# Block products in the first pass over d_ff for groups 3, 4 and 5

## The chip, the cores and the metric

The kernel runs on one core of one Trainium2 chip. The metric is the time of one execution on the device in microseconds. Each time shown is of one whole execution; the profile is of one further execution, whose span is counted from its first instruction to its last. The engines are TensorE (PE, with its weight loads as PEld), VectorE (DVE), ScalarE (ACT), GpSimd (POOL) and SyncE (SP), which issues all of this kernel's DMAs.

## The reference

The first half is an attention over 4 batches, 8 heads, 768 positions and 64 columns per head. A query sees the keys less than 16 positions away (local part) and, in the same softmax, 24 summaries of the whole sequence: the maximum of the keys and the mean of the values of each block of 32 positions, with log(32) added to the scaled score. The heads are joined to x, 3072 tokens by 512 columns. The second half is a feed-forward layer:

```
h = x @ w_in                                      # 512 -> 2048
g = np.maximum(h, 0.0) + np.log1p(np.exp(-np.abs(h)))   # softplus
return (g @ w_out).astype(np.float32)             # 2048 -> 512
```

q, k, v and w_in come with eight times their plain spread. w_in and w_out reach the kernel as 64-bit numbers, which it turns into float32 on the chip.

## The kernel before

**Precision.** A float32 matrix is kept as two parts in the type float32r, high and low (a rounded copy and the rest). A product of two such matrices is three matmuls, high x high, high x low and low x high (TERMS).

**Tokens and groups.** The 3072 tokens are twelve chunks of 256 (CH), two to a group: six groups of 512 tokens (x = 0 to 5). d_ff is sixteen blocks of 128 (f = 0 to 15), of which the first eight are one half (HALF). Only half of the weights lies in SBUF at a time, so the phases are: groups 0 to 4 with the first half, group 5 with the first half and then the second, and groups 4 to 0 with the second. After a first pass, po (512 tokens by 512 columns in PSUM) goes to DRAM as "part", and x as "raw"; the second pass loads both again (attended, reload).

**Attention** of a chunk (attention, L605) goes by two pairs of heads: scores (PE, L629), mask and maximum (DVE, L642), exponential (ACT, L650), inverse sums (DVE), normalise (POOL, DVE or ACT, L663, L666), transpose by blocks on DVE (L696) and through DRAM (L704, L708), values (PE, L727, into xo, a PSUM bank of the ring "ph"). For groups 1 to 4 xo is copied to a block r (L739), kept in DRAM, and split into high and low parts of whole x (prepare_whole, L813 and L820). For groups 0 and 5 it is split straight from the bank (L757, L761). The attention of a group stands in the order beside the products of the one or two groups ahead of it.

**Plain products.** hidden (L1036) makes h of one f: 12 matmuls of 512 columns, in two tasks h0 and h1 (L1045). The result has one of the two PSUM banks of the ring "ph".

**Block products.** hidden_pair (L1062) makes h of two f at once. x is seen as 2 by 2 blocks (chunk by half of d_model), and so is the w_in of the two f. Seven products of blocks, six matmuls of 256 columns each (L1085; a11, s3, s2, s1, a12, s4, a22), take the place of eight; seven combinations on DVE (L1095) and a copy of one product (p1, L1104 or L1105) put them together in two banks, z and y, which the pair holds both. It needs seven operands of x: blocks 0, 1, 3 and x12's and others' differences (prepare, L834: less is a subtraction, L797 or L798; split is a high part, L782, and a low part, L789), in places x0 to x2 (two buffers each) and x3 to x6 (one each). And it needs four sums of blocks of w_in (sums_of_weights, L968: joined L985, combined L993 to L996, high L1009, low L1016), in places s0 to s3.

**After h**: high part of softplus (gh, L1147), exact softplus in place in the bank (L1151), rest (gl, L1155), and the projection to po (L1162), per f 8 matmuls with gh and 4 with gl, or, for the first and last f of a pass, 3 for each of four groups of 128 tokens.

**Where block products are used before**: "pairs = f0 > 0" (L1124), so in the second passes of groups 4 to 0 alone. The sums of w_in are made for the second half only (arrive, L1281).

**Order.** Every task (a matmul chain, an operation on an engine, a DMA) is declared with what it reads and writes; SEQUENCE, a list of task numbers written out by hand in the file, gives the order in which all are issued (Order.issue), and each engine and SP's queue run their tasks in that order. A letter behind a number picks another engine for a task (ways). Buffers of the ring "t" (two), and banks of "ph" (two), are given out in the order of the sequence.

The first task numbers of the sequence are those of the start: constants, 40 matmuls on ident, the first keys and values (declare_first, declare_first_values, L412), where six loads of v (L423) go through the ring "gh" of four buffers and are summed on PE (L428).

Of the kernel before, what the change touches and what calls it, by code (L numbers as in the profile page):

```python
# [147 lines left out]
0 3 4 162 43 1 5 6 51 7 44 8 9 10 11 12 13 14 15 16 17 18 19 20 21 22 23 24 25 26 27 28 29 30 31 32 33 153 45 47 68  # L148
154a 158a 34 155 163a 64 46 52 156 53 55 164 2 157 165 167a 72 54 35 57 189 69 36 159 59 160a 161 49 73 48 37 86 313
61 166 56 74 171 87 190 38 39 168 75 58 40 191 88 41 60 104 62 100 76a 172a 50 152 321a 180 192 176a 77 79 66 316 65  # L150
173 174 63 67 169 42 78 108 71 175 80 170 70 177 314 315 185 194 101 109 89 312 193 110 122 123 81 324 208 198 181a
103 90b 124 107 105 343 111 82 195 84 344 182 209a 91 102 136 106 196a 112a 346 183 199 184 92 93 94 95 325 83 213
178a 197 85 342 113 125 326 372 345 96 186 210 211 114 179 351 212 138 115 116 98 117 99 97 376 126b 127 317 118 120
327 214 200a 129 128 215a 130 354 137 217 131 373 246 218 380 328 329 134 330 140 132 121 141 355 133 320 119 135 201
247 319 356 248 390 255 249 392 393 331 223a 357 187 389 334 332 318 374 322 333 391 202 204 250 256 257 188 262 203
139 258 323 216a 358 259 359 263 227 219a 377 264 251 269 270 252 205 146a 398a 271 384 360 378 265 206a 401 375 220
272 253 266 228a 335 347 350 232 353 221 254 260 402 336 273 381 361 420 229 423 421 143 276 362 363 348 230 364 419
385 403 277 349 422 283 352 338 261 222 379a 382 404 386 284 231 428 278 236 279 237 207a 280 405b 267 431 285 286 365
233 406 407 234 515 366 516 224 268 274 287 432 433 238a 368a 235 383a 290 387a 394 291 408 396 388 225 292 149a 434
239 240 520a 517 297 241 410 411 400 397 340 409 275 298 226 435a 436 242 523 299 293 395 281 399 693 542 243 294 282  # L160
# [73 lines left out]
def kernel(  # L234
# [639 lines left out]
    def weights(pair):  # L874
# [6 lines left out]
        for outer, which in tiles:  # L881
# [81 lines left out]
            )  # L963


    s_bufs = {}

    def sums_of_weights(f):  # L968

# [365 lines left out]
```

## Time and profile before

| | us |
|---|---|
| three runs | 633.65, 633.3, 628.66 |
| median | 633.3 |
| the profiled execution, whole | 630.05 |
| its span | 628.3 |
| mean granted clock of TensorE | 0.983 of full speed |

The page of the profile gives the busy time of each engine, and the chain that ended last followed back from the last instruction. A window of the profile gives the busy time of each engine in a stretch of the span, so a stage can be read by itself. The boundaries of the stages, from PE's instructions in the order of the sequence: group 0's products begin at 51.9 us, group 1's at 110.1, group 2's at 164.0, group 3's at 215.0, group 4's at 270.8, group 5's at 323.8 and its second half at 362.6; the block products of group 4 begin at 406.0, of 3 at 446.4, of 2 at 490.4, of 1 at 530.8 and of 0 at 572.2. A matmul's duration in the profile is longer than the spacing of matmuls, as they overlap; the spacing is read from the chain of waits, which counts them.

### The profile page before, as it was taken

The numbers are of one execution on the slowest core, as the hardware profiler recorded it, in microseconds if no ns is written. First come the engines' busy times: TensorE is split into PE (matmuls) and PEld (weight loads), VectorE is DVE, ScalarE is ACT, GpSimd is POOL, SyncE is SP. The second block draws the span as 40 slices with busy tenths as digits, with TensorE's granted clock in tenths as the row PEclk, the third lists the DMA queues.
The fourth block names the chain that finished last, engine by engine and source line by source line (L and its number), as shares of the span: only waits on it lengthen the run. The fifth ranks groups of instructions, "written<-read, shape, count | busy, mean of one in ns | idle before, by whom it ended". The sixth has DMA issues, their size and how long they took to land.

```text
span 628.3 us, 12022 instructions
## 1 busy us (share of the span) xinstructions
PE 609.2 (97%) x4452; PEld 508.9 (81%) x4452; DVE 388.0 (62%) x998; ACT 328.0 (52%) x809; POOL 162.0 (26%) x145
## 2 busy tenths in 40 slices
PE   8769999999999999999999999999999999999997
PEld 7557777788888878877888888899889899898995
DVE  5887997764457454535427979764557557655442
ACT  2898895965766676456526677441323122222220
POOL 3325435132213043002003443490111403002000
PEclk9868999999999999999999999999999999999999
DMA  9998887989998887885634632103122050030301
GB/s 303 265 272 268 254 264 233 262 261 231 272 263 253 259 268 220 254 236 158 212 116 155 222 127 84 34 34 118 51 76 78 17 185 1 35 100 1 104 32 67
DMA packets 88955, 104.39 MB, mean 166 GB/s; under 512 B 27489, under 2 KB 67009, under 8 KB 88129
## 3 DMA queue, kind: packets, MB, share of 16 engines
q1 hardware_dynamic: 88896, 103.62, 54.5%
q8 instruction: 35, 0.57, 0.4%
q14 instruction: 24, 0.19, 0.1%
HBM read 73.92 MB, written 27.26 MB: 161 GB/s over the span
## 4 chain that ended last, share of the span: by engine, by line
PE 85%; DMA 8%; SPq 3%; ACT 1%; DVE 1%; issue 1%; DVEq 0%; POOL 0%; POOLq 0%; ACTq 0%
PE po L1162 40%; PE ph L1045 21%; PE hx L1085 9%; PE hy L1085 7%; PE xo L727 3%; PE sc L629 3%; DMA raw<-w_in_dram 2%; DMA k<-kT_dram 2%; DMA squares<-tb 2%; PE warm L1236 2%; DMA kf<-kT_dram 1%; DMA q<-qT_dram 1%; DMA v<-v_hp_dram 1%; SPq L708 1%; SPq L523 1%
## 5 line engine op out<-in xcount | busy, mean ns | idle before, releaser
L1162 PE MATMUL po<-w,gh 128*128 128x512 f32 x768 | 204.2, 394 | 0.0
L1162 PEld LDWEIGHTS po<-w,gh 128*128 128x128 f32 x768 | 141.4, 188 | 30.6 <-issue 0.6
L1045 PE MATMUL ph<-xw,w 128*128 128x512 f32 x672 | 163.9, 395 | 2.1 <-DVE gl L1155 2.0
L1045 PEld LDWEIGHTS ph<-xw,w 128*128 128x128 f32 x672 | 125.6, 188 | 32.5 <-DVE gl L1155 2.8
L1162 PE MATMUL po<-w,gl 128*128 128x512 f32 x384 | 116.6, 397 | 0.0
L1162 PEld LDWEIGHTS po<-w,gl 128*128 128x128 f32 x384 | 70.9, 188 | 15.9 <-issue 0.5
L650 ACT ACTIVATE sp<-sp,nm 128x120 f32<-128x120 f32 x192 | 73.1, 382 | 5.9 <-DVE nm L642 5.7
L1147 ACT ACTIVATE gh<-hx 128x512 fp32r<-128x512 f32 x20 | 12.0, 599 | 114.9 <-DVE hx L1095 114.9
L948 POOL TENSOR_TENSOR t<-t,raw 128x1024 int32<-128x1024 int32 (+1 forms) x20 | 42.4, 2122 | 98.8 <-DVE t L934 28.4
L1155 DVE TENSOR_TENSOR gl<-ph,gh 128x512 fp32r<-128x512 f32 x56 | 38.0, 684 | 40.8 <-ACT ph L1151 39.3
L1147 ACT ACTIVATE gh<-ph 128x512 fp32r<-128x512 f32 x56 | 33.5, 598 | 53.4 <-PE ph L1045 48.5
L789 POOL TENSOR_TENSOR x<-r,x 128x512 fp32r<-128x512 f32 x18 | 24.5, 1370 | 82.0 <-ACT x L782 32.2
L642 DVE CUSTOM_DVE_ANT_0 sp<-sc,added 128x120 f32<-128x120 f32 x192 | 40.8, 277 | 4.9 <-PE sc L629 3.9
L663 POOL TENSOR_TENSOR sp<-sp,ss 128x960 f32<-128x960 f32 x10 | 18.4, 1843 | 87.6 <-DVE ss L658 62.8
L650 ACT ACTIVATION_READ_ACCUMULATOR sp<-sp,nm 128x1 f32 x192 | 36.0, 187 | 0.0
L1085 PE MATMUL hx<-x,sw 128*128 128x256 f32 x240 | 35.4, 283 | 0.0
L1085 PE MATMUL hx<-x,w 128*128 128x256 f32 x240 | 35.1, 282 | 0.0
L1085 PEld LDWEIGHTS hx<-x,w 128*128 128x128 f32 x240 | 32.8, 189 | 1.9
L696 DVE STREAM_TRANSPOSE tb<-sp 128x1024 f32<-128x1024 f32 x20 | 24.8, 1242 | 15.2 <-POOL sp L663 7.9
L1085 PE MATMUL hy<-x,sw 128*128 128x256 f32 x240 | 33.2, 282 | 0.0
L1151 ACT ACTIVATE ph<-ph 128x512 f32<-128x512 f32 x56 | 32.8, 591 | 0.0
L1085 PEld LDWEIGHTS hx<-x,sw 128*128 128x128 f32 x240 | 31.7, 189 | 0.5
(108 smaller groups left out, 821.6 us busy)
## 6 DMA issues: line engine op xcount, KB each, us to landing
squares<-tb SPq DMA_DIRECT2D x20, 512.0 KB
pT<-squares SPq DMA_DIRECT2D x80, 128.0 KB
raw<-w_out_dram SPq DMA_DIRECT2D x16, 512.0 KB
kf<-kT_dram SPq DMA_DIRECT2D x16, 384.0 KB
raw<-w_in_dram SPq DMA_DIRECT2D x6, 1024.0 KB
q<-qT_dram SPq DMA_DIRECT2D x20, 256.0 KB
raw<-r SPq DMA_DIRECT2D x20, 256.0 KB
part<-ob SPq DMA_DIRECT2D x10, 512.0 KB
```

What stands on the lines that cost most here:

```text
L629: nc.tensor.matmul(unit(g * NU + h * NPAIR + i)[r * QW:(r + 1) * QW, k0:k1], lhsT=q[rows, w * QW:(w + 1) * QW], rhs=k[rows], start=True, s ...
L642: nc.vector.tensor_tensor_reduce(out=sp()[:, n], in0=unit(n), in1=added()[:, kinds.index((lows[w], lows[w + 1]))], scale=-SCALE, scalar=FL ...
L650: nc.scalar.activation(sp()[:, n], sp()[:, n], AF.Exp, bias=nm()[:, n:n + 1], scale=-1.0, accum_out=ss()[:, n:n + 1],)
L696: nc.vector.transpose(out=tb().rearrange("p k (u q) -> p u k q", q=SQ), in_=tiles.sp().rearrange("p u (k q) -> p u k q", q=SQ),)
L789: engine.tensor_tensor(to(1), a(), to(0).bitcast(F32), op=ALU.subtract)
L948: nc.gpsimd.tensor_tensor(a, a, word(0, I32), op=ALU.add)
L1045: nc.tensor.matmul(ph(), lhsT=lhs(part, cc), rhs=xw[cc][0]()[:, xw[cc][1], a], start=cc == 0 and n == 0, stop=cc == NCC - 1 and n == 2,)
L1085: nc.tensor.matmul(to()[:, half], lhsT=lhs(wa, cc), rhs=of_x(xa)[:, cc * CH:(cc + 1) * CH], start=cc == 0 and m == 0, stop=cc == NG - 1 an ...
L1147: nc.scalar.activation(gh(), all_of(), AF.Softplus)
L1151: nc.scalar.activation(all_of(), all_of(), AF.Softplus)
L1155: nc.vector.tensor_sub(out=gl(), in0=all_of(), in1=gh().bitcast(F32))
L1162: nc.tensor.matmul(po[t](), lhsT=a()[:, t * P:(t + 1) * P], rhs=w2()[:, part, i2 * DM:(i2 + 1) * DM], start=f == f0 and i == 0, stop=f == ...
```

## The change

SEVEN = 3 parts the groups. Groups 0 to 2 are as before in their first pass: plain products from whole x. Groups 3 and 4 use block products in the first pass too. Group 5 uses them for the first half of d_ff, and for the second half plain products made from four blocks (hidden_blocks): 24 matmuls of 256 columns per f in place of 12 of 512. The three groups' x is therefore prepared as seven operands in the first pass (prepare); group 5 also keeps the block x12 by itself ("single", in a buffer of the place x0), and its xo is copied to r like the others'.

The sums of w_in are now made for the first half as well (tasks z0 to z6, declared after the attention of group 3), in s0 to s3; the keys and values that are loaded for the summaries of batch 3 (kf, st) go to the ring "t" from then on. The first six loads of v use the places r0 to r2, two buffers each, in place of the ring "gh". The sequence is written anew: 2260 tasks in place of 2099. Up to the last products of group 1 PE, ACT and SP have the same order as before.

```diff
--- before.py
+++ after.py
...
@@ -324,6 +331,7 @@
     phases = [(x, 0, HALF) for x in range(NX - 1)] + [(NX - 1, 0, NF)]
     phases += [(x, HALF, NF) for x in reversed(range(NX - 1))]
     BLOCKS = (0, 1, 2, 3)
+    SEVEN = 3
 
 
     def scratch(f, name):
@@ -359,8 +367,12 @@
             n_t = BLOCK // NHP
             rows = v_hp[self.b].rearrange("hp (n t) c -> (hp n) t c", t=BLOCK)
             for i in range(NHP):
-                kf = buffer([P, S], F32, "kf", tag=f"s{i % 2}", pool=wts, bufs=1)
-                st = buffer([P, n_t, P], F32, "st", tag=f"s{2 + i % 2}", pool=wts, bufs=1)
+                if s_bufs:
+                    kf = buffer([P, S], F32, "kf", "t", T_BUFS, dynamic=True)
+                    st = buffer([P, n_t, P], F32, "st", "t", T_BUFS, dynamic=True)
+                else:
+                    kf = buffer([P, S], F32, "kf", tag=f"s{i % 2}", pool=wts, bufs=1)
+                    st = buffer([P, n_t, P], F32, "st", tag=f"s{2 + i % 2}", pool=wts, bufs=1)
 
                 def load_k(i=i, kf=kf):
                     nc.sync.dma_start(out=kf(), in_=kT[self.b, i])
@@ -416,7 +428,7 @@
             kept = block(3, "v0")
             self.first_v = kept
             for i in range(S // P):
-                part = buffer([P, DM], F32, "vn0", tag="gh", bufs=NU)
+                part = buffer([P, DM], F32, "vn0", tag=f"r{i // 2}", bufs=2)
 
                 def load_v(i=i, part=part):
                     src = v_hp[self.b, :, i * P:(i + 1) * P].rearrange("hp s c -> s hp c")
@@ -446,7 +458,7 @@
                 order.add(SP, 0.4, keep, [self.first_v], [(self.v, hp)], size=12 * KiB, row=512)
 
 
-    x_bufs = {}
+    x_bufs, s_bufs = {}, {}
 
     def x_of(x):
         if x not in x_bufs:
@@ -732,7 +744,7 @@
 
         order.add(PE, 1.2, values, [pT, *((pT, k) for k in range(NSQ)), *tiles.v_keys], [xo])
 
-        if x and x < NX - 1:
+        if x and (x < NX - 1 or x >= SEVEN):
             r = block(2 * i + hp // NG)
 
             def take(copy):
@@ -842,6 +854,9 @@
         elif n == 2:
             less(r12, r11, r11)
             split(r11, *operand(x, 2), NG * CH)
+            if x == NX - 1:
+                held = single[x] = buffer([P, 2, NG, CH], F32R, "x", tag="x0", bufs=2)
+                split(r12, lambda part: held()[:, part].rearrange("p g c -> p (g c)"), (held,), NG * CH)
         else:
             split(r22, *operand(x, 3), NG * CH)
             less(r22, r12, r12)
@@ -963,18 +978,14 @@
             )
 
 
-    s_bufs = {}
-
     def sums_of_weights(f):
 
 
-        order.group = f"s{f}"
+        order.group = f"s{f}" if f >= HALF else f"z{f}"
         a = buffer([P, 2, 2, CH], F32, "ws", "t", T_BUFS, dynamic=True)
         sw = s_bufs[f] = sums_of(f % HALF // 2, "sw")
         held = list(dict.fromkeys(w_in_of[f + k][0] for k in range(2)))
         begun = [order.writer[w, part] for w in held for part in range(2)]
-        if f == HALF - 2:
-            begun.append(products[-1])
         for k, w in enumerate(held):
             n = 2 // len(held)
 
@@ -1033,7 +1044,39 @@
         w, i, n = w_in_of[f]
         return w, lambda part, cc: w()[:, part, (cc * n + i) * P:(cc * n + i + 1) * P]
 
+    single = {}
+
+    def hidden_blocks(x, f):
+
+        w, lhs = of_w(f)
+        ph = bank([P, CT], "ph")
+        x12 = single[x]
+        blocks = {(0, 0): operand(x, 0), (0, 1): operand(x, 1), (1, 1): operand(x, 3)}
+        blocks[1, 0] = (lambda part: x12()[:, part].rearrange("p g c -> p (g c)")), (x12,)
+
+        def product(i):
+            for hp in range(2):
+                of_x = blocks[i, hp][0]
+                for cc in range(NG):
+                    for n, (part, a) in enumerate(TERMS):
+                        nc.tensor.matmul(
+                            ph()[:, i * CH:(i + 1) * CH], lhsT=lhs(part, hp * NG + cc),
+                            rhs=of_x(a)[:, cc * CH:(cc + 1) * CH],
+                            start=hp == cc == n == 0, stop=hp == 1 and cc == NG - 1 and n == 2,
+                        )
+        for i in range(2):
+            task = order.add(
+                PE, 1.43, lambda i=i: product(i),
+                [(*blocks[i, hp][1], part) for part in range(2) for hp in range(2)] + [(w, part) for part in range(2)],
+                [ph],
+            )
+            if not i:
+                first_after(task)
+        return [ph]
+
     def hidden(x, f):
+        if x >= SEVEN:
+            return hidden_blocks(x, f)
 
         w, lhs = of_w(f)
         xw = whole_x(x)
@@ -1121,11 +1164,12 @@
 
     def feed_forward(x, f0, f1):
         po = [buffer([P, DM], F32, "po", "po", NT, psum) for _ in range(NT)]
-        pairs = f0 > 0
+        plain = range(HALF, NF) if x == NX - 1 else range(HALF) if x < SEVEN else ()
         for f in range(f0, f1):
             if f0 == 0 and f == HALF:
                 arrive(range(HALF, NF))
             order.group = f"f{x}.{f}"
+            pairs = not (f0 <= f < f1 and f in plain)
             if not pairs:
                 hs, n = hidden(x, f), 0
             elif f % 2 == 0:
@@ -1139,7 +1183,7 @@
             gh = buffer([P, CT], F32R, "gh", bufs=4)
             gl = buffer([P, CT], F32R, "gl", bufs=4)
 
-            def all_of(h=h):
+            def all_of(h=h, pairs=pairs):
                 return h().rearrange("p n c -> p (n c)") if pairs else h()
 
 
@@ -1263,6 +1307,9 @@
                 r[n] = attention(x, i, hp, Places(c, hp, sums, pads), False)
                 if x < NX - 1:
                     keep(x, n, r[n])
+                if x >= SEVEN:
+                    prepare(x, n, r)
+                elif x < NX - 1:
                     prepare_whole(x, n, r)
         return sums
 
@@ -1289,6 +1336,9 @@
     for x, f0, f1 in phases:
         if x and not f0:
             sums = attend(x, sums)
+            if x == SEVEN:
+                for f in range(0, HALF, 2):
+                    sums_of_weights(f)
         elif f0:
             attended(x)
         feed_forward(x, f0, f1)
```

More of the change, by code (lines that the diff above doesn't have):

```diff
@@ L147 @@
 SEQUENCE = """
[L148 to L157, printed above, removed]
@@ new lines @@
+1068 861 881 884 882 888 1069 862 885 1042 889 1021 1022 866 592 1208 890 1002 867 1029 1043 1003 1070 1031 1209 893
+896 1046 1032 1224 894a 1045 1210 895 899 897 904 898 1223 902 900 976 906 1023 1035 905 1005a 903 901 907 886 1211
+908 913 1212a 1006 887 1228 1044 1225 909 1034 914 977a 910 891 1030 915 978 1231 1071 1047 622 1247 1213 1232 1255
+1048 1050a 1051a 1233 1072 892 1058 1073 1075 1064 918 1059 921 920 924 919a 922 1060 1061 927 929 925 923 1214 930
+931 928 933 1074 932 926 934 1234 911 912 938 939 1235 916 935 940 1052a 812 1063 1246 1049 1076 1077 917 1249 1004
@@ new lines @@
+936 1084 1081 1079 1085 1087 1215 1086a 1082 1250 1080a 1088 1236 1089a 1083 1090 1096 1091 1203 1093 1094 1248 1092
+1101 1095 1099 1097 1204 1098 1102 1103 1100 1104 937 1258 1105 1112 1106 1107 1113 1114 942 692 1216 941 1117 1217
+1120 1123 1259 1119 1277 1276 1118a 1121 1122 1126 1128 1124 943 1129 1130 1278 944 1127 945a 946 1132 1131 948 1133
+1125 1207 1137 1237 1280 1279 1108 1206 1138 1285 1218 1134 1139 949a 1109 1288 1219 1078 1238 1260 950 1220a 1261
+1110 1142 1145 1262 1143a 1146 1148 1144 1153 1241 1147 1226 1227 1588 1239 1229 1149 1151 1263 1264 1111 1155 1152
@@ new lines @@
+1460 1426 1427 1390 1393 1446 1428 1394 1456 1396 1400 1471 1398 1399 1401 1402 1472 1447 1461a 1448 1465 1397 1429
+1457a 1509 1403 1473 1404 1405 1383 1409 1387 1410 1406 1488 1458 1388 1478 1411 1449 1475 1462 1489a 1493 1479 1490
+1430a 1407 1408 1491 1524 1525 1531 1526 1532 1492 1431 1527 1463 1412 1464 1476 1533 1466 1413 1528 1529 1728 1497
+1494 1512 1538 1539 1534 1467 1477 1480a 1535 1530 1545 1540 1546 1536 1541 1468 1542 1547 1498 1552 1548 1549 1495
+1481 1496 1499a 1482 1483 1500 1537 1510 1553 1501 1554 1484 1559 1543 1555 1560 1561 1502 1562 1503a 1556 1485 1544
@@ new lines @@
+2140 2129 2143a 2018 2013 2015 2014 2016 2023 2019 2017 2021 2020 2025 2024 2022 1953 2026 2027 2028 2029 1954 2034
+2035 1973 2036 2039 2042 2045 2040a 2043 1974 2046 1981 2041 1988 1980 2044 2047 2050 1987 2048 1989 1978 2051 2049
+1979 1983 2054 2052 2055 1984 2030 2056 1985 2031 2053 2059 2032 2060 2033 2061 2037 2064 2067 2066 2065a 2068 2070
+2073 2069 2071 2075 2072 2077 2074 2076 2038 2078 2079 2080 2057 2084 2081 2085 2086 2058 2089 2116 2120 2092 2095
+2090 2141a 2093 2142a 2091 2100 2096 2138 2094 2098 2097 2135a 2102 2139 2062 2136a 2101 2144 2099 2103 2104 2105
```

138 lines of the change are left out of this document (66 added, 72 removed), and 3 rows, old and new, of the table SEQUENCE.

## The prediction

> **What bounds the kernel now.** I read the page first, then the busy time by stage, then the chain of waits in order of time, and last the timeline of single hand-overs.
>
> ```profile
> span 628.3 us, 12022 instructions
> PE 609.2 (97%) x4452; PEld 508.9 (81%) x4452; DVE 388.0 (62%) x998; ACT 328.0 (52%) x809; POOL 162.0 (26%) x145
> PE 85%; DMA 8%; SPq 3%; ACT 1%; DVE 1%; issue 1%; DVEq 0%; POOL 0%; POOLq 0%; ACTq 0%
> ```
>
> TensorE is the bound: 85% of the chain that ended last. The rest of that chain lies in the start. The stages show it; the columns are the stretch, its length, and the busy time of PE, PEld, DVE, ACT and POOL with instruction counts, then the granted clock, the DMA share and GB/s.
>
> ```profile
> 164.00:215.00 51.00, 51.00 (x411) 41.08 (x409) 28.05 (x99) 32.77 (x92) 12.04 (x14) 1.00 0.87 259
> 215.00:271.00 56.00, 56.00 (x462) 45.00 (x459) 29.13 (x110) 38.37 (x117) 13.85 (x15) 1.00 0.85 253
> 271.00:324.00 53.00, 51.98 (x386) 41.56 (x385) 22.42 (x68) 25.69 (x65) 5.85 (x5) 1.00 0.58 172
> 324.00:363.00 39.00, 39.00 (x170) 31.70 (x169) 28.43 (x41) 23.24 (x34) 13.25 (x9) 1.00 0.55 192
> 363.00:406.00 43.00, 43.00 (x188) 34.96 (x187) 38.08 (x46) 29.12 (x38) 17.32 (x9) 1.00 0.20 68
> 406.00:446.00 40.00, 40.00 (x256) 36.31 (x255) 23.18 (x47) 14.29 (x26) 19.42 (x15) 1.00 0.24 83
> ```
>
> These are the products of groups 2, 3 and 4, then group 5's two halves, then the first group in block products. PE is busy all through at the full clock, whether the stage works with plain products (up to 406) or with block products (after it). So time falls where PE's own work falls, unless a wait takes its place. In these stages one wait of PE is on record:
>
> ```profile
> PE sc L629 <- ACT gh L1147: 1.0, 1, 1.0
> ```
>
> **The change part by part. Products of groups 3, 4 and 5, first half.** The chain of waits gives what a matmul costs when PE runs without a gap (start, length, what, count):
>
> ```profile
> 122.97 0.98 PE sc L629 x32
> ...
> 129.42 5.55 PE ph L1045 x24
> 134.97 0.93 PE po L1162 x4
> 409.18 1.43 PE hx L1085 x12
> ```
>
> Two plain blocks of d_ff are 24 matmuls of 512 columns: 5.55 us, 0.231 each. A block product is 6 of 256 columns: 1.43/2 = 0.713. A pair by blocks takes 7 of them, 4.99, so it saves 0.56. Three groups have four pairs each in the first half: 12 x 0.56 = 6.7 us off PE.
>
> **Group 5, second half.** hidden_blocks does a plain block of d_ff as 24 matmuls of 256 columns in place of 12 of 512: 24 x 0.119 = 2.86 against 5.55/2 = 2.775, 0.08 more, for eight blocks 0.65 us. PE's net saving is 6.7 - 0.65 = 6.05 us.
>
> The Trainium skill ("TensorE: Matmul & The Clock Gate", Back-to-back issue gap) puts the warm spacing of matmuls at columns / 2.4 GHz plus about 2.5 ns. By that a 512-column matmul would take 0.216 and a 256-column one 0.109, and the net saving would be 12 x 0.59 - 8 x 0.03 = 6.8 us; the rows have 0.231 and 0.119, and they decide.
>
> **The start.** The six v loads of batch 0 (L423) move from the ring of four "gh" buffers to six places of r0 to r2. The queue of SP, in order of time:
>
> ```profile
> 10.77 0.43 SPq L557 DMA_DIRECT2D first<-v_hp_dram  x1
> 12.32 0.38 SPq L423 DMA_DIRECT2D vn<-v_hp_dram  x1
> 13.31 0.43 SPq L497 DMA_DIRECT2D k<-kT_dram  x1
> 14.60 0.37 SPq L423 DMA_DIRECT2D vn<-v_hp_dram  x1
> ```
>
> and the stretch around them, in the columns of the stages:
>
> ```profile
> 10.00:15.00 5.00, 5.00 (x84) 3.15 (x84) 4.97 (x15) 0.45 (x3) 1.34 (x1) 1.00 1.14 345
> ```
>
> Loads 5 and 6 wait for the matmuls that free the first two buffers: SP stands 12.32 - 11.20 = 1.12 and 14.60 - 13.74 = 0.86 us. Up to well past them the written order is the same before and after, so the change is worth between 0 and 1.98 us here. The DMA engines are full then (share 1.14 in the last row), so an earlier issue mostly queues: I take 0.5.
>
> **Operands and sums: the other engines.** Groups 3, 4 and 5 now make seven operands each (group 5 one more, "single"), where before they split whole x; each pair adds seven combinations on DVE; and four sums of w_in are made in group 2's stage. The rows for these:
>
> ```profile
> L739 DVE COPY r<-xo 128x512 f32<-128x512 f32 x8 | 5.5, 689 | 9.3 <-PE xo L727 9.3
> L797 DVE TENSOR_TENSOR r<-r 128x512 f32<-128x512 f32 x10 | 6.9, 687 | 1.4 <-POOL x L789 1.2
> L789 DVE TENSOR_TENSOR x<-r,x 128x512 fp32r<-128x512 f32 x17 | 13.6, 810 | 0.9 <-ACT x L782 0.9
> L782 DVE CAST x<-r 128x512 fp32r<-128x512 f32 x14 | 5.8, 425 | 3.0 <-PE ph L1045 1.5 <-PE hx L1085 1.5
> L789 POOL TENSOR_TENSOR x<-r,x 128x512 fp32r<-128x512 f32 x18 | 24.5, 1370 | 82.0 <-ACT x L782 32.2 <-ACT gh L1147 25.8 <-DVE x L782 24.0
> L993 DVE TENSOR_TENSOR ws<-ws 128x256 f32<-128x256 f32 x3 | 1.3, 418 | 0.0
> L994 DVE TENSOR_TENSOR ws<-ws 128x256 f32<-128x256 f32 x3 | 3.4, 1132 | 0.1
> L995 DVE TENSOR_TENSOR ws<-ws 128x256 f32<-128x256 f32 x3 | 1.3, 424 | 0.1
> L996 DVE TENSOR_TENSOR ws<-ws 128x256 f32<-128x256 f32 x3 | 2.3, 750 | 0.1
> L952 DVE CAST w<-t 128x1024 fp32r<-128x1024 f32 x6 | 4.1, 677 | 0.0
> L663 DVE TENSOR_TENSOR sp<-sp,ss 128x960 f32<-128x960 f32 x9 | 11.3, 1256 | 0.2
> L1016 DVE TENSOR_TENSOR sw<-ws,sw 128x1024 fp32r<-128x1024 f32 x2 | 2.6, 1302 | 0.0
> ```
>
> In the new order group 2's stage has on DVE three of the four combinations of sums (L993 to L996: 2.72 each), two joins (two additions of the size of L797, 1.37, and about 0.8 for the half as wide one), two low parts (1.30 each) and four casts (the cast of the same form in L952, 0.68 each): 8.2 + 2.2 + 2.6 + 2.7 = 15.7 us. Group 3's operands bring it two subtractions, four low parts and a cast (4.9 us), and five casts and three low parts of half that width go (at half the rows, 2.3). Two more normalisations stand on DVE rather than ACT (L663, 1.26 each). 28.05 + 15.7 + 2.6 + 2.5 = 48.9 of 51 us, 96%. Between 363 and 406 DVE stood at 38.08 of 43, 89%, and PE did not wait: I take nothing here, and give it as a rival below.
>
> The keys and values of batch 3 (eight loads, kf and st) leave places of their own for the two buffers of the ring "t", beside outputs and sums. SP issues in order: where such a load waits for a buffer, the loads of the next attention stand behind it, and after them the transpose through DRAM, and PE's values. The DMA engines have room there (share 0.58 to 0.87), so I take 0 and leave this to the upper bound.
>
> **The hand-over between pairs.** A pair holds both PSUM banks of the "ph" ring until its last softplus and rest are done. The shortest case in the second passes:
>
> ```profile
> 548.57 0.88 PE L1085 MATMUL hy<-x,w 128*128 128x256 f32 x6
> 549.57 0.42 DVE L1095 TENSOR_TENSOR hy<-u,hy 128x256 f32<-128x256 f32 x1
> 550.09 0.60 ACT L1147 ACTIVATE gh<-hy 128x512 fp32r<-128x512 f32 x1 [0.41 <-DVE hy L1095]
> 550.58 0.59 ACT L1151 ACTIVATE hy<-hy 128x512 f32<-128x512 f32 x1
> 551.21 0.69 DVE L1155 TENSOR_TENSOR gl<-hy,gh 128x512 fp32r<-128x512 f32 x1 [0.62 <-ACT hy L1151]
> 552.06 0.88 PE L1085 MATMUL hx<-x,w 128*128 128x256 f32 x6
> ```
>
> The product's six matmuls leave PE at 548.57 + 0.71 = 549.28, the bank is free at 551.90: 2.6 us, which PE fills with other matmuls. In the new order I summed PE's work between a pair's last product and the next user of a bank, with po at 0.93/4 per matmul and scores at 0.98. All pairs of groups 3 and 4 have 3 us or more; group 5's first has 2.1 (three tokens of po, 0.70 each), and two of those three need that pair's own gh and gl: with one product and one token of cover, 1.4 us, against 2.6 from its last product on z, PE stands 1.2 us.
>
> **The hand-over between groups.** After the last values of group 5 PE has only two tokens of po (1.4 us) and three products (2.1) before the product on operand 4, and one more, at 4.2 us, before that on operand 5. DVE must by then do the copy to r (0.69), three subtractions (0.69 each) and three low parts (0.69 to 0.81): 4.8 to 5.2 us. PE stands 0.6 to 1.0. Operand 6 has a cast on DVE (0.43) and a low part on POOL (1.37) after these, due 1.4 us later: 0.4 more. I take 1.2 together. From group 3 to 4 the same count leaves 0.1 to 0.3, from 2 to 3 nothing, because projections of the group before lie between: 0.2.
>
> Sum of new waits: 1.2 + 1.2 + 0.2 = 2.6, between 0 and 6 (each of twelve pairs losing 0.5). The wait of 1.0 at a5's scores may go or stay; I leave it. Kernel: -6.05 - 0.5 + 2.6 = -3.95 us.
>
> **The rivals.** (a) All of the saving arrives: the new stages run like those after 406, where no hand-over cost anything, the start gives its 1.98, and the 1.0 wait is gone: -6.05 - 2 = -8, about 625. For it: everywhere but at group 5's first pair PE's cover of 3 us exceeds 2.6. Against it: the counts for group 5.
>
> (b) DVE bounds group 2's stage. L993 and L994 have the same form, but 418 against 1132 ns, L996 750: an instruction on the sums sometimes takes 0.3 to 0.7 us more. POOL's work in that stage (12.04 before) gains three joins, a combination, two low parts of sums and five steps on operands. Were eight of DVE's instructions there held by 0.7, DVE would have 48.9 + 5.6 = 54.5 us where PE has 51, and PE would lose 3.5 us more than forecast: -0.45, about 632.8. The Trainium skill ("SBUF — State Buffer", Who interferes with whom) says that VectorE with two SBUF inputs and GpSimd exclude each other for a whole instruction; the rows above agree that something like it occurs.
>
> (c) Slower: softplus queued behind the exponentials. Attention still runs beside groups 3 and 4, and ACT works in order:
>
> ```profile
> L650 ACT ACTIVATE sp<-sp,nm 128x120 f32<-128x120 f32 x192 | 73.1, 382 | 5.9 <-DVE nm L642 5.7
> L1147 ACT ACT_TABLE_LOAD x21 | 26.9, 1283 | 4.9 <-PE ph L1045 4.5
> ```
>
> One exponential task is 73.1/24 = 3.05 us, with the table load that softplus needs after it 1.28. If it stands ahead of a pair's gh, the bank is free after 2.6 + 4.3 = 6.9 us in place of 2.6, where PE's cover is 3 to 4.6: 2.3 to 3.9 us lost. With plain products ACT's gh came late for PE once, by 1.0 (the wait above); one bank was then still free, while a pair holds both. Six such tasks fall in groups 3 and 4. From two on the saving is gone; if all six hit and group 5 loses its 2.4, it is -6.55 + 6 x 3.1 + 2.4 = +14, about 647. In the order they mostly stand behind p1, early in a pair, which speaks against.
>
> **How the numbers follow.** The profiled execution took 630.05 us (span 628.3), the three runs 628.66 to 633.65, median 633.3. My -3.95 makes 626.1 of the first and 629.35 of the median; the runs scatter by more than the change, and the profiled one and the lowest lie 3 to 5 below the median, so I say 628.5. About 1% (6.3 us) is what a measurement of this kernel can tell from none. Chances: forecast 0.43, (a) 0.30, (b) 0.17, (c) 0.10. Faster by over 1% means below 627.0: nearly all of (a), 0.27, and a quarter of the forecast, 0.11, make 0.38; slower by over 1%, above 639.6: (c) mainly, 0.10; between, 0.52. The range: (a) from the median, 625.3, less some 3 for the scatter, 622.5; up to (b), 632.8, and 2 for the scatter, 635.
>
> **What would show it.** The rows of L1085 by form should grow from 840 to 1344 matmuls, and the wide ones of L1045 fall from 672 to 288, with 192 of 256 columns in hidden_blocks. The stages of groups 3 to 5 should be about 2 us shorter each in PE's work. SP's two stops on L423 should be gone. Waits of PE at the first pair of group 5, on DVE and ACT, confirm the 2.4; none there means (a). PE waiting on DVE in group 2 means (b); a bank wait on gh behind L650 means (c). I am wrong in kind if 256-column matmuls on new operands are spaced wider than 0.119, or if PE's clock falls below 1.00 after 110 us.

## The result: slower by 0.9%

The changed kernel takes 635.99 us (median of 10 runs, 633.34 to 638.59) against 630.11 for the kernel before (10 runs, 628.18 to 633.65). The ratio is 1.0088, with a 95% interval of 1.0059 to 1.0116: some 5.5 us more, where the prediction had 4 us less. The profiled execution is the fastest of the ten, 633.34 us with a span of 631.6, so its trace can explain 3.3 us of the loss; what the other runs add, the experiments show in part.

### The profile page after: what moved, and what is told of

The parts are those of the page before. It is cut to its first block, busy times and chain, and to the rows that moved or that the text cites. A ratio compares the mean times of both kernels' runs of the same rounds, so it can differ in the third digit from the quotient of the medians.

```text
span 631.6 us, 12806 instructions
## 1 busy us (share of the span) xinstructions
PE 607.7 (96%) x4764; PEld 517.9 (82%) x4764; DVE 434.3 (69%) x1097; ACT 347.0 (55%) x830; POOL 200.8 (32%) x173
## 4 chain that ended last, share of the span: by engine, by line
PE 76%; DMA 7%; DVE 7%; ACT 6%; SPq 3%; issue 1%; POOL 0%; DVEq 0%; POOLq 0%; ACTq 0%
PE po L1206 37%; PE hx L1128 14%; PE hy L1128 10%; PE ph L1088 5%; PE ph L1062 4%; PE xo L739 3%; ACT sp L662 2%; PE sc L641 2%; DMA squares<-tb 2%; DMA raw<-w_in_dram 2%; DMA part<-ob 1%; DMA k<-kT_dram 1%; DMA first<-qT_dram 1%; DVE sp L654 1%; ACT sp L678 1%
## 5 line engine op out<-in xcount | busy, mean ns | idle before, releaser
L1088 PE MATMUL ph<-xw,w 128*128 128x512 f32 x288 | 71.7, 398 | 3.8 <-DVE gl L1199 2.1
L1088 PEld LDWEIGHTS ph<-xw,w 128*128 128x128 f32 x288 | 53.3, 188 | 18.9 <-DVE gl L1199 3.8
L810 POOL TENSOR_TENSOR r<-r 128x512 f32<-128x512 f32 x19 | 25.4, 1340 | 107.5 <-DVE x L801 60.7
L1128 PE MATMUL hx<-x,sw 128*128 128x256 f32 x384 | 57.4, 285 | 0.9 <-ACT p L1147 0.6
L1128 PE MATMUL hx<-x,w 128*128 128x256 f32 x384 | 56.4, 282 | 1.5 <-DVE u L1138 1.4
L1128 PEld LDWEIGHTS hx<-x,w 128*128 128x128 f32 x384 | 52.2, 189 | 5.1 <-DVE u L1138 1.6
L1128 PE MATMUL hy<-x,sw 128*128 128x256 f32 x384 | 53.1, 282 | 0.0
L1128 PEld LDWEIGHTS hx<-x,sw 128*128 128x128 f32 x384 | 50.1, 188 | 2.6 <-ACT p L1147 1.0
L1128 PEld LDWEIGHTS hy<-x,sw 128*128 128x128 f32 x384 | 49.0, 188 | 0.6 <-DVE u L1138 0.3
L794 ACT CAST x<-r 128x512 fp32r<-128x512 f32 x40 | 24.1, 619 | 41.5 <-PE hy L1128 10.9
```

What stands on the lines that cost most here:

```text
L794: copy(out=to(0), in_=a())
L810: ways=[Way(POOL, pool(NG * CH), lambda: nc.gpsimd.tensor_tensor(to(), a(), b(), op=ALU.subtract))],
L1088: nc.tensor.matmul(ph(), lhsT=lhs(part, cc), rhs=xw[cc][0]()[:, xw[cc][1], a], start=cc == 0 and n == 0, stop=cc == NCC - 1 and n == 2,)
L1128: nc.tensor.matmul(to()[:, half], lhsT=lhs(wa, cc), rhs=of_x(xa)[:, cc * CH:(cc + 1) * CH], start=cc == 0 and m == 0, stop=cc == NG - 1 an ...
```

## The profile after the change

The first lines of the page and its chain of waits by engine:

```profile
span 631.6 us, 12806 instructions
PE 607.7 (96%) x4764; PEld 517.9 (82%) x4764; DVE 434.3 (69%) x1097; ACT 347.0 (55%) x830; POOL 200.8 (32%) x173
...
PE 76%; DMA 7%; DVE 7%; ACT 6%; SPq 3%; issue 1%; POOL 0%; DVEq 0%; POOLq 0%; ACTq 0%
```

PE's share of the chain fell from 85% to 76%. DVE and ACT, 1% each before, have 7% and 6%: PE now waits for them. The stages again, in the columns of the prediction: groups 1, 2, 3 and 4, then the two halves of group 5, each from its first product to the next one's.

```profile
110.10:164.90 54.80, 53.73 (x475) 42.56 (x474) 35.06 (x122) 39.65 (x117) 18.72 (x22) 1.00 0.93 260
164.90:219.00 54.10, 52.60 (x439) 40.85 (x438) 43.89 (x132) 38.89 (x107) 18.96 (x15) 1.00 0.87 260
219.00:272.30 53.30, 51.32 (x489) 44.36 (x488) 37.85 (x116) 38.60 (x103) 24.84 (x25) 1.00 0.88 236
272.30:325.20 52.90, 52.90 (x471) 45.89 (x469) 31.68 (x90) 26.34 (x68) 9.96 (x7) 1.00 0.52 160
325.20:367.10 41.90, 40.97 (x256) 36.17 (x255) 37.32 (x74) 30.28 (x44) 15.97 (x11) 1.00 0.65 217
367.10:408.60 41.50, 41.50 (x274) 37.94 (x273) 36.19 (x37) 30.02 (x39) 24.52 (x15) 1.00 0.15 52
```

Group 1 of the kernel before, which the prediction did not show:

```profile
110.10:164.00 53.90, 53.90 (x478) 43.26 (x477) 33.05 (x112) 39.02 (x118) 13.03 (x14) 1.00 0.92 255
```

PE, which was busy all through groups 1 to 3, now stands for 1.07, 1.50 and 1.98 us there, and 0.93 us in group 5. A busy PE can still hide short stops between matmuls. So I took from each stage's length its matmuls at the spacings of the prediction (0.231 wide, 0.119 narrow; 32 scores 0.98, 32 values 1.08, from the chain of waits), and what is left is lost time (us):

| stage | before: length, lost | after: length, lost |
|---|---|---|
| group 0 | 58.2, 5.6 | 58.5, 5.9 |
| group 1 | 53.9, 1.0 | 54.8, 2.7 |
| group 2 | 51.0, 0.8 | 54.1, 3.8 |
| group 3 | 55.8, 1.1 | 53.3, 3.9 |
| group 4 | 53.0, 2.3 | 52.9, 1.4 |
| group 5, both halves | 82.2, 0.0 | 83.4, 2.0 |
| five second passes | 217.4, 0.3 | 218.8, 1.7 |

Lost time grew by 10.2 us, PE's work fell by 5.9, the start gained 0.3: the last matmul starts 4.0 us later, and 0.7 of that comes back in the tail. One profile's lost time is rough: in group 0, whose work no experiment changes, it lies between 5.1 and 9.1 us in the sixteen profiles. But in groups 1 to 3 together it is 2.9 us before and 10.3 after, and it stays between 2.9 and 5.2 in the three profiles with the order of before (with experiments 11 and 14) and between 8.9 and 14.7 in all the others. PE's work itself is as forecast. The groups of matmuls by form:

```profile
L1128 PE MATMUL hx<-x,sw 128*128 128x256 f32 x384 | 57.4, 285 | 0.9 <-ACT p L1147 0.6 <-DVE hx L1138 0.3
L1128 PE MATMUL hx<-x,w 128*128 128x256 f32 x384 | 56.4, 282 | 1.5 <-DVE u L1138 1.4
L1128 PE MATMUL hy<-x,sw 128*128 128x256 f32 x384 | 53.1, 282 | 0.0
L1128 PE MATMUL hy<-x,w 128*128 128x256 f32 x192 | 28.2, 283 | 0.0
...
L1088 PE MATMUL ph<-xw,w 128*128 128x512 f32 x288 | 71.7, 398 | 3.8 <-DVE gl L1199 2.1 <-DVE r L751 1.1 <-DVE xw L773 0.6
L1062 PE MATMUL ph<-x,w 128*128 128x256 f32 x192 | 24.0, 282 | 0.0
```

1344 block matmuls, 288 wide ones of x and 192 narrow ones in their place, exactly the counts forecast. And PE's waits between 150 and 340 us, from the timeline:

```profile
155.63 3.04 PE L1088 MATMUL ph<-xw,w 128*128 128x512 f32 x12 [1.07 <-DVE r L751]
...
182.33 4.71 PE L1088 MATMUL ph<-xw,w 128*128 128x512 f32 x18 [0.35 <-DVE gl L1199]
...
191.69 1.15 PE L739 MATMUL xo<-pT,v 120*64 120x64 f32 x32 [1.15 <-DVE gl L1199]
...
222.08 1.18 PE L1128 MATMUL hx<-x,sw 128*128 128x256 f32 x6 [0.57 <-ACT p L1147]
...
236.44 0.98 PE L1128 MATMUL hx<-x,w 128*128 128x256 f32 x6 [1.42 <-DVE u L1138]
...
329.62 0.98 PE L1128 MATMUL hx<-x,sw 128*128 128x256 f32 x6 [0.34 <-DVE hx L1138]
...
332.97 0.51 PE L1206 MATMUL po<-w,gl 128*128 128x512 f32 x1 [0.48 <-DVE gl L1199]
```

Only the last two lie where I had looked. Behind the first wait, in group 1, DVE had this:

```profile
151.87 1.25 DVE L708 STREAM_TRANSPOSE tb<-sp 128x1024 f32<-128x1024 f32 x1 [3.88 <-DMA squares<-tb]
153.26 0.28 DVE L654 CUSTOM_DVE_ANT_0 sp<-sc,added 128x120 f32<-128x120 f32 x1
...
154.89 0.69 DVE L751 COPY r<-xo 128x512 f32<-128x512 f32 x1
```

DVE stood 3.88 us until the one buffer tb was stored to DRAM; then came the transpose, a mask of eight parts, and only then the copy that frees the bank for which PE waited. In the kernel before, ACT had made this copy 3.5 us earlier:

```profile
151.35 0.59 ACT L739 COPY r<-xo 128x512 f32<-128x512 f32 x1 [1.92 <-PE xo L727]
```

So ACT's order is the same as before only up to this copy, not up to the last products of group 1. In group 2 the first join of the sums stood the same way, on DVE and on POOL, for the ring "t":

```profile
178.75 1.30 DVE L996 TENSOR_TENSOR ws<-w 128x256 f32<-128x256 f32 x2 [3.10 <-DMA part<-ob]
178.87 1.78 POOL L996 TENSOR_TENSOR ws<-w 128x256 f32<-128x256 f32 x2 [13.48 <-DMA part<-ob]
```

And in group 3, behind a mask, the copy p1 stood behind an output copy that waited for the same ring:

```profile
234.90 0.69 DVE L1240 COPY ob<-po 128x512 f32<-128x512 f32 x1 [0.69 <-DMA part<-ob]
235.51 0.41 DVE L1148 COPY p<-hx 128x256 f32<-128x256 f32 x1
```

The second passes, in which nothing was edited, lost 1.4 us more without a wait. Their projections of gh follow each other (mean from start to start between 410 and 600 us, worked out from the trace) at 232.1 ns where they were at 229.2, those of gl at 231.7 after 233.1; the first passes show the same shift. In the second passes that makes 320 x 2.9 - 160 x 1.4 ns = 0.7 us, half of what they lost; where the other half comes from no run shows. Twenty projections in a row on the chain of waits, before and after:

```profile
536.13 4.59 PE po L1162 x20
```

```profile
539.68 4.65 PE po L1206 x20
```

## The experiments

Three theories at first: Q, steps that the change adds or moves stand in front of what PE needs next, in the queues of DVE and SP; H, a pair's own hand-over of its two banks; P, the place of the gh buffers, which lost their first user (the v loads) and with it perhaps their address. Times are medians; the kernel before had 630.3 (1 to 4), 629.7 (5 to 8), 631.1 (9 to 11), 630.8 (12) and 630.9 (13, 14) beside them. Most edits below move the time by 1 to 2 us, and the interval of every single edit that lowered the ratio (2, 3 and 6 to 9) overlaps the changed kernel's, 1.0059 to 1.0116; only all of it together (10, 12 and 13) is clear of it.

### 1. The v loads back

```diff
-                part = buffer([P, DM], F32, "vn0", tag=f"r{i // 2}", bufs=2)
+                part = buffer([P, DM], F32, "vn0", tag="gh", bufs=NU)
```

Loads 5 and 6 are issued right behind the two sums that free their buffers; the rest of the order stays.

> The changed kernel with only the six v loads of batch 0 put back into the four gh buffers (loads 5 and 6 wait for the first two sums again). Theory P (places): the projections of gh in the second passes went from 229.2 to 232.1 ns each in the changed kernel although nothing was edited there; if the place of the gh buffers is the cause, 1152 projections fall back by 2 to 3 us in all and the time by as much less the 0.3 us that the start had gained: about 633.5. Theory Q (queue on DVE: sums of w_in and operands stand in front of a pair's rest and of the mask) and theory H (a pair's own hand-over of banks): only the start's 0.3 us comes back, 636.3.

637.8 us, ratio 1.0098 (1.0064 to 1.0132): no gain. But the spacing of gh went back to 229.1 ns and that of gl to 233.0, and the second passes lost 1.0 us where they had lost 1.7. The first user of the buffers does set the spacing. The total hides it, since this profile's start is 1.8 us later (53.42 after 51.64) and its groups 1 to 3 lost 1.7 us more. Experiments 7 and 11 move no other step, so that the start does not hide it.

### 2. The sums left out

```diff
-        sw = s_bufs[f] = sums_of(f % HALF // 2, "sw")
+        own = f >= HALF
+        sw = s_bufs[f] = sums_of(f % HALF // 2, "sw") if own else w_in_of[max(f, 2)][0]
...
-            copy(out=to(0), in_=whole())
+            if own:
+                copy(out=to(0), in_=whole())
...
```

(and so for joins, combinations and low parts: the block products of the first passes read w_in itself, and only the work of making the sums is missing).

> The changed kernel with the four sums of the first half of w_in left out (joins, combinations, casts and low parts; the block products of the first passes read rows of w_in in their place, so the results are wrong and every matmul, load and operand step stays). Theory Q: the sums and their wait for the ring t hold DVE in group 2's stage; its time above PE's own work falls from 3.8 to about 1 us and group 3's (3.9) by 1, so -4: 632. Theory H: the sums were hidden, within 0.5 of 636.0. Theory P: 636.0.

636.7 us, 1.0078 (1.0047 to 1.0110). Group 2's stage fell as theory Q said, to 52.30 us with 2.0 lost after 3.8. The time did not follow. In this profile group 1, before the sums, took 57.2 us: PE's wait for the copy r was 2.00 us rather than 1.07, and the twelve matmuls behind it took 4.47 us rather than 3.04. That led to experiment 9.

### 3. Four operands in place of seven

```diff
+    x_bufs, s_bufs, second, MADE = {}, {}, set(), {2: 0, 4: 0, 5: 1, 6: 3}
...
     def operand(x, n):
+        n = n if x in second else MADE.get(n, n)
```

(Subtractions, casts and low parts of operands 2, 4, 5 and 6 are not done in first passes; the products read other operands in their place.)

> The changed kernel with the combined operands left out in the first passes of groups 3, 4 and 5: operands 2, 4, 5 and 6 are the tiles of operands 0, 0, 1 and 3, and their subtractions, casts and low parts are not done (results wrong; all matmuls and sums stay). My term of 1.2 + 0.2 us for the hand-over between groups goes if it was there: -1.4 to 634.6. Theory Q in its second half (operand steps queued in front of a pair's rest and of the masks, in groups 3 to 5): -3 to 633. Theory H (banks only) and theory P: within 0.5 of 636.0.

636.0 us, 1.0081 (1.0054 to 1.0109): nothing measurable. The wait for p1 at the first pair of group 3 (0.57) is gone, as it is in some profiles that make all operands (1, 4, 5 and 6); a wait at its second pair (0.98) and those of 0.34 and 0.49 at group 5's first pair stay: they are the pairs' own hand-over, not the operands'. Group 5's first half lost 1.5 us rather than 1.9. Of my term of 1.2 for its operands 0.4 at most shows, and even that is not clear of the scatter: with all operands made, experiment 7 has 1.7 there and experiment 2 has 2.7.

### 4. An eighth product

```diff
-                for cc in range(NG):
+                for cc in [*range(NG)] * (2 if a == "s1" and f < HALF else 1):
```

> The changed kernel with the product s1 done twice in each of the twelve new pairs (result right): 12 x 0.713 = 8.56 us more of PE's work, so that a pair costs PE more than two plain blocks. If PE sets the time in these stages the time grows by 8.6 to 644.5, and the saving of the seventh product was worth its full price. If the pairs wait for DVE or ACT anyway (theories Q and H), the eighth product falls into waits in part: +4 to +6, 640 to 642.

642.6 us, 1.0181 (1.0144 to 1.0219): 5.9 us more than the changed kernel by the ratios, 6.6 by the medians, for 8.56 us of work, 69 to 78%. The two intervals leave about 3 us either way, but the profile agrees: the stages of groups 3 to 5 are 6.7 us longer in it. So PE still sets the time in these stages. The saving was not lost because it lay beside the bound. It was there, and something else was added.

### 5. The order of before, up to group 2's first product

The first 658 words of the order are those of the kernel before, each step on the engine it had there; the rest follows in the changed order.

> The changed kernel, whose written order up to group 2's first product (658 of 2260 steps) is taken from the kernel before, each step on the engine it had there; from there on the changed order. Nothing that the change adds lies in this part. Theory R (the order was written anew everywhere, and its first part is worse: DVE waits 3.9 us for the store of the transposed block at 152, and PE 1.2 to 2.2 us behind it): group 1's stage returns from 54.8 to 53.9 or less and the start of group 2 comes 1 to 3 us earlier: 633 to 635. Theory L (loss lies only where the new work is, groups 2 to 5): within 0.5 of 636.0.

639.0 us, 1.0139 (1.0109 to 1.0169), worse than either. The matmuls that fill group 1's stage in the changed kernel took 53.96 us rather than 54.8 (the kernel before's 53.9 hold three wide matmuls more). So only about half of what this stage had lost came back, less than theory R had it. Group 2's stage takes 58.6 from its first product: steps of group 3's attention that the changed order does earlier were now late, PE waited 1.64 and 3.60 us for them, and the clock fell during the second wait. What the first part of the order is worth by itself this run does not show.

### 6. The sums in other buffers

```diff
-        a = buffer([P, 2, 2, CH], F32, "ws", "t", T_BUFS, dynamic=True)
+        place = "t" if f >= HALF else "x1" if f in (0, 6) else "x2"
+        a = buffer([P, 2, 2, CH], F32, "ws", place, 2, dynamic=True)
```

> The changed kernel with the sums of the first half of w_in made in idle buffers of x1 and x2 instead of the two buffers of ring t; nothing else. Theory T (ring t): DVE's wait of 3.1 us at the first join for the store of group 1's outputs goes, and with it PE's waits of 0.5 to 0.9 and part of the 1.3 in group 2's stage: -1.5, group 2's stage 52.5 after 54.05, 634.5. Theory D (DVE is simply full there, 43.9 of 54 us in bursts): -0.3 at most, 635.7.

634.3 us, 1.0069 (1.0044 to 1.0094); the interval overlaps the changed kernel's, the profile does not. Group 2's stage:

```profile
168.40:220.40 52.00, 52.00 (x440) 41.04 (x439) 44.91 (x124) 39.38 (x108) 20.07 (x16) 1.00 0.91 272
```

PE is busy all through, while DVE does more than in the changed kernel (44.91 us). The waits at 182 and 191 are gone, as they are in experiment 2. So these two came from the ring, not from DVE's load. This profile has the long wait in group 1, too, and shows what it costs:

```profile
157.52 4.61 PE L1089 MATMUL ph<-xw,w 128*128 128x512 f32 x12 [2.13 <-DVE r L751]
```

```profile
157.50:162.20 4.70, 4.68 (x14) 3.69 (x14) 2.74 (x8) 4.32 (x18) 1.70 (x4) 0.64 0.78 216
```

The granted clock of those 4.7 us is 0.64, and twelve matmuls take 4.61 us, not 3.04.

### 7. Four v loads in gh, two in r2

```diff
-                part = buffer([P, DM], F32, "vn0", tag=f"r{i // 2}", bufs=2)
+                part = buffer([P, DM], F32, "vn0", tag="gh", bufs=NU) if i < NU else buffer([P, DM], F32, "vn0", tag="r2", bufs=2)
```

> The changed kernel with four of the six v loads of batch 0 in the gh buffers and two in r2, so that no load waits and gh is again the first buffer placed. If the place of gh sets the spacing of its matmuls, the 768 wide projections of gh come at 229 instead of 232 ns and those of gl at 233 instead of 231.7: -2.2 + 0.5 = -1.7 us, 634.3, with the start as in the changed kernel. If the start's wait made the spacing in the first experiment (another phase of the clock), spacing stays at 232 and the time at 636.0.

633.7 us, 1.0055 (1.0035 to 1.0076): 2.1 us less than the changed kernel by the ratios, about what the spacing makes (1.7, worked out below). The spacing is 229.2 and 233.0 ns, and the twenty projections:

```profile
541.93 4.61 PE po L1211 x20
```

### 8. p1 on ACT, ahead of the exponentials

Three words of the order move: 869 is p1 (a letter means the other engine), 1067 the exponentials, 690 the output copy, 873 the second combination:

```diff
-690a 1067 1000 868 871 874 870 985 989 1205a 986 869a 872 873
+1000 868 869 1067 871 874 870 985 989 1205a 986 872 873 690a
```

> The changed kernel with three steps moved at group 3's second pair: the copy p1 goes from DVE, where it stands behind a mask and an output copy that waits for ring t, to ACT ahead of the exponentials of that mask, and the output copy goes behind the pair's second combination. Theory H (a pair's first product is held by its own copy, as the bank stays taken): PE's wait of 1.2 to 1.8 us before product a12 goes: -1.4, 634.6. Theory L2 (something later waits in its place, as the exponentials start later): within 0.4 of 636.0.

634.1 us, 1.0061 (1.0038 to 1.0084), a median as theory H expected. The wait of 1.42 before a12 is gone; one of 0.52 for p1 stands at s2. But this profile has a wait of 1.19 at values ahead of it, and group 3's stage is no shorter (53.9 after 53.3), so where the time was gained it does not show.

### 9. The copy first

```diff
-727 751 566a 591a
+591a 727 751 566a
```

(591 is the copy r of group 2's third part, 727 the transpose, 751 the mask.)

> The changed kernel with one step moved: in group 1's stage DVE copies the values of attention out of their PSUM bank before the transposed block and the mask, not behind them (both stand behind the store of the block before). The wait of PE there was 1.07 us in the changed kernel's profile and 1.3 to 2.1 us in eight others with the same order; after six of the seven waits of 1.8 us and more the granted clock stood at 0.50 for about 3 us, after none of the shorter ones. Theory C (a wait of about 2 us costs the clock too): the wait goes, and with it the half clock between 155 and 165 us: 1.1 to 2.1 of wait, and 1.6 us for the clock where it fell: -2.5, 633.5. Theory W (the wait moves to the next thing that the late block holds, the scores or the values of group 3): within 0.7 of 636.0.

635.6 us, 1.0072 (1.0053 to 1.0090). The wait is gone, and group 1's stage is at the kernel before's level with a full clock; but group 2's grew:

```profile
111.30:165.10 53.80, 53.66 (x476) 42.67 (x475) 34.07 (x111) 38.63 (x115) 18.47 (x21) 1.00 0.91 260
165.10:220.70 55.60, 52.79 (x439) 40.77 (x438) 44.99 (x141) 39.92 (x110) 18.86 (x15) 1.00 0.88 258
```

PE waits there for a low part of x (0.59), for the transposed block (0.49), and for gl (0.57 and 1.15). Both theories (C and W) hold in part: during the old wait some of these later steps had been done unseen.

### 10. All of it together

Experiments 6, 7, 8 and 9, and one load of batch 3's values (word 1013) behind the last return of the transposed block (973).

> The changed kernel with all that helped: four v loads in gh and two in r2, the sums in x1 and x2, p1 of group 3's second pair on ACT, the copy of the values first in group 1's stage, and the second load of batch 3's values behind the last part of the transposed block that it delays (issue order of SP). If the waits add up: -2.1 - 1.2 - 1.7 - 2.5 - 0.5 = -8.0, 628, just below the kernel before at 630. If they cover for each other (one gone, the next late step waits at the same place): half of it, 632.

632.6 us, 1.0024 (0.9999 to 1.0048): 4.0 us of the 5.5 are back, two thirds of what the four gave one by one (1.2 + 2.1 + 1.7 + 1.0 = 6.0 by their ratios, each uncertain by more than its size). This is the one result on the whole loss that is clear of noise. The profile does not show the gain: it is of a long execution (637.05 us), with a wait of 2.32 us at the values of group 3's second part and the clock halved behind it.

### 11. The kernel before, its v loads in r

```diff
-                part = buffer([P, DM], F32, "vn0", tag="gh", bufs=NU)
+                part = buffer([P, DM], F32, "vn0", tag=f"r{i // 2}", bufs=2)
```

> The kernel before with only its six v loads of batch 0 moved from gh to r0, r1 and r2, as in the changed kernel. Theory P (place): without a change to any matmul the wide projections of gh go from 229.2 to 232.1 ns and those of gl from 233.1 to 231.7, and the wide products of the first passes with them or not; 768 x 2.9 - 384 x 1.4 = +1.7 us, less 0.3 to 1 for the start: about 631 against 630.0. Theory S (the spacing comes from the changed order of PE): spacing stays at 229.2 and the time falls by 0.3 to 1.

633.4 us, 1.0035 (1.0018 to 1.0052): the kernel before gets 2.2 us slower by this line alone. Its spacing goes to 232.1 and 231.9 ns, with no matmul moved:

```profile
537.54 4.63 PE po L1162 x20
```

With experiment 7 this shows the spacing from both sides. By the spacing, 768 x 2.9 - 384 x 1.4 ns, the line should cost 1.7 us, where I had put it down as a gain of 0.5. Experiment 14 asks what else is in the 2.2.

### 12 and 13. More of the same

Experiment 10 and four steps moved (words 1015, 1016, 654 and 624); then five more (the returns 729 to 732 behind 720, and product 874 ahead of 871).

> The last but one kernel (all that helped together, 632.6) with four more steps moved in group 2's stage, where PE still stood 2.3 us before the values of group 3's second part, with half clock after it: the load of a third part of batch 3's keys goes behind the loads of those values, DVE's maximum over it behind the rests of two blocks, one rest ahead of a transposed block, and a low part of group 2's x ahead of a mask. Theory Q (loads and DVE steps of later work stand in front of what PE needs next): the wait of 2.3 and the clock's 1.5 go, -2 to -4: 629 to 630.5, level with the kernel before. Theory M (DMA and DVE are full there, another wait comes in its place): 632 to 633.

> The twelfth kernel (632.4, level with before) with two more repairs: the four returns of the transposed block of group 3's first part go ahead on SP's queue, as they stood in the kernel before (issued at 164 to 170 there, at 172 to 174 in the changed kernel, with the values that need them at 177 in both), and product s1 of group 3's second pair goes ahead of s2, so that PE has a product that needs nothing of p1. Theory Q: PE's wait of 1.9 at those values and of 0.5 at s2 goes: -2.4, 630.0, under the kernel before (630.8) by a little. Theory M (DMA is full in group 2's stage, the wait goes elsewhere): 632 to 632.8.

632.4 us, 1.0017 (0.9987 to 1.0046), level with the kernel before; then 633.7 us, 1.0031 (1.0008 to 1.0054). The wait that the moves were meant for went from 2.32 to 1.91 and then 0.87 us, and new ones stand elsewhere. In experiment 13:

```profile
179.34 1.15 PE L739 MATMUL xo<-pT,v 120*64 120x64 f32 x32 [0.87 <-DVE gl L1200]
...
188.87 1.05 PE L641 MATMUL sc<-k,q 64*64 64x120 f32 x32 [0.77 <-DMA q<-qT_dram]
...
216.05 1.15 PE L739 MATMUL xo<-pT,v 120*64 120x64 f32 x32 [1.33 <-DVE gl L1200]
```

This fits theory M: with the DMA engines at 0.87 to 0.93 in these stages and DVE's bursts on top, a step moved ahead puts another behind. No run tests it by itself. No version beat the kernel before.

### 14. The kernel before, without SP's stops

```diff
-                part = buffer([P, DM], F32, "vn0", tag="gh", bufs=NU)
+                part = buffer([P, DM], F32, "vn0", tag="gh", bufs=NU) if i < NU else buffer([P, DM], F32, "vn0", tag="r2", bufs=2)
```

> The kernel before with its six v loads of batch 0 in four gh buffers and two of r2: gh stays the first buffer placed, and SP's two stops of 1.12 and 0.86 us on these loads are gone. My term for the start alone: 0 to -1.98, taken -0.5: 630.3 against 630.8 for the kernel before. If the DMA engines were full there (share 1.14 between 10 and 15 us), 0.

632.8 us, 1.0022 (1.0000 to 1.0045): no gain, and 1.4 us more by the ratio, though the spacing stays at 229 and 233 ns. Group 0's first product starts 0.96 us earlier (50.98 after 51.94), about half of the bound of 1.98, and at 95 us PE gives it back:

```profile
95.15 0.64 PE L629 MATMUL sc<-k,q 64*64 64x120 f32 x16 [1.96 <-DMA k<-kT_dram]
```

The scores of group 2 wait for keys, and the clock is halved behind the wait. The kernel before waits 0.54 there, the changed kernel 0.76, others up to 2.45. So experiment 11's 2.2 us need not be the spacing alone: by the ratios it lies only 0.8 above this run, which has the loads moved but not the spacing, and the two intervals overlap. The times price the line at 2 us; how much of that is the spacing is known by the 1.7 worked out from it.

## Why the prediction was wrong, point by point

- **PE's work, -6.05: right.** Counts and spacings as forecast, 5.9 by the trace, and experiment 4 shows that PE's work still counts for most of its price, 69 to 78%.
- **The start, -0.5: wrong in its sign.** I looked at the queue that the six loads leave and not at the ring that they leave. With them as first user the matmuls of gh come at 229 ns, without them at 232: 1.7 us by the spacings, 2.1 and 2.2 by the times of experiments 7 and 11, of which the second may hold something else (experiment 14). What the queue gave, 0.3 us at group 0's first product, is gone at group 1's (110.10 after 110.13).
- **"The DMA engines have room there, so I take 0" for ring "t": wrong.** The room was in the engines, not in the ring. A join waited 3.10 us for a store with DVE's queue behind it, and an output copy 0.69 with p1 behind it. With the sums in other buffers the waits of PE behind the join are gone (experiment 6); the times of experiments 6 and 8 are 1.2 and 1.7 us lower (the second moves a mask, too), neither clear of noise by itself.
- **DVE at 96% of group 2's stage, "I take nothing": the number was too high, the nothing too low.** DVE stood at 43.89 of 54.1 us, 81%. The share of a stage said little either way: with 44.91 busy in experiment 6 PE did not wait, since the sums no longer waited for the ring. Rival (b) named the right stage and nearly the size (3.5; lost time there grew by 3.0). What it gave as cause is there, but smaller. Beside POOL's work four of DVE's instructions in this stage took longer than their like elsewhere, 2.8 us in all where (b) had 5.6. The clearest is one that takes 0.17 otherwise:

```profile
186.04 1.54 POOL L801 TENSOR_TENSOR x<-r,x 128x512 fp32r<-128x512 f32 x1 [5.39 <-ACT x L794]
...
186.36 1.25 DVE L669 TENSOR_SCALAR ss<-ss 128x8 f32<-128x8 f32 x1
```

In experiment 6 the same instruction took 1.26 us and PE did not wait, so this is not what made PE stand.

- **Waits at group 5, 2.4: size right, half the cause wrong.** Lost time in its two halves grew by 2.0. The first pair's own hand-over is there (0.34 and 0.48 in the rows, the rest in shorter stops); of the 1.2 for the operands experiment 3 shows 0.4 at most.
- **Pairs of groups 3 and 4, whose cover of 3 us was to exceed the 2.6 of a hand-over: wrong for group 3.** The 2.6 was the shortest case of the second passes, with nothing in front of it on DVE. In group 3 the copy p1 and the combinations behind it stood in line, PE waited 0.57 and 1.42 us, and lost time grew by 2.8 where I had nothing. In group 4, where I had 0.2, it fell (1.4 after 2.3).
- **Stages that the change does not touch, 0: wrong.** The order was written anew from group 1 on. In it a copy that frees a bank went from ACT to DVE and stood there behind a transpose and a mask. The wait was 1.07 us in the profile after and 1.3 to 2.1 in the seven others with this order; lost time in group 1 grew by 1.7.
- **The clock, 1.00 after 110 us: my sign of being wrong in kind.** It held in the profile after and fell, after 110 us, in seven of the fourteen others (2 to 7 and 10), below. I had no term for it.
- **Rival (c)**, softplus behind exponentials, did not show: none of PE's waits quoted here ends on gh behind exponentials. What was slow is (c)'s pattern in another place, p1 behind a mask.
- **Rival (a)'s sum** leaves out a term that it names: with the wait of 1.0 gone it is -6.05 - 1.98 - 1.0 = -9.0, not -8.

In all: the one gain was priced rightly, and costs of 1.7, 3.0 and 2.8 us of lost time in groups 1, 2 and 3, and of 1.7 us by the spacing (in part in these stages), were put at nothing or as a gain, because DVE, the DMA engines and PE's cover had room on average. Three repairs of the order and the ring, one moved load and the spacing are together worth 4.0 of the 5.5 us, some 2 either way; how the 4.0 divide among them is known only roughly. What stays open is how much of the remaining loss in groups 1 to 3 the amount of work forces, and how much the order; experiments 12 and 13 stop at a draw.

## What to carry to other kernels

Price a rewritten order as a part of the change: look, stage by stage, for what stands ahead of each copy that frees a bank, and for steps that wait on a store while others queue behind them; the share of busy time of a stage tells neither. When a buffer gets another first user, compare the spacing of matmuls that nobody touched. And where PE is the bound, count a wait of 2 us or more as almost twice its length, for the clock can fall behind it.

## What the runs showed of the hardware

**A wait of PE of about 2 us can halve the clock.** In the profiles of the fourteen experiments and of the changed kernel, between 60 and 240 us, PE stood 1.8 us or longer 13 times. After ten of them (1.82 to 3.60 us) the granted clock was 0.50, mostly for about 3 us; after three (1.89, 1.91, 2.07) it stayed at 1.00, as it did after every shorter wait (up to 1.64). At half clock 3 us are worth 1.5: twelve matmuls took 4.61 us rather than 3.04. The Trainium skill ("TensorE: Matmul & The Clock Gate", Why this matters for your kernels) warns of idle gaps above about 3 us; here 1.82 us was enough. As the wait in group 1 lies between 1.07 and 2.13 us from profile to profile, it makes part of the changed kernel's scatter.

**Another first user of a buffer changes the spacing of matmuls.** Moving the first user of gh, without touching a matmul, moved the 768 matmuls that read gh from 229.2 to 232.1 ns and the 384 that read gl from 233.1 to 231.7, in both kernels and both directions, and each of the sixteen profiles goes by it. That the buffers' address does it is argued, as no trace holds addresses; nor does any run show which property of it would.
